# Attention scores of 20 of 32 visits: from float32 products of 64 rows to float32r products of rounded and remaining parts

## The chip, the cores and the metric

The kernel runs on one core of a Trainium2 chip. The metric is device time in microseconds (us) of one execution; the kernel before takes 1064.93 us (median of 3 runs, 1064.68 to 1065.62). The engines are called PE (TensorE; PEld is its weight load), DVE (VectorE), ACT (ScalarE), POOL (GpSimd) and SP (SyncE, which issues all the DMAs here).

## What is computed

Attention with a compressive memory for 4 batches, 8 heads, 576 tokens and 64 dimensions, and behind it two feed-forward layers over 2304 tokens of 512 values:

```python
scores = scale * np.matmul(q, k.transpose(0, 1, 3, 2))      # causal, then softmax
local = np.matmul(a, v)
mem_out = mem_ret / mem_norm                                # phi(q) against M_prev, z_prev
attn = g * mem_out + (1 - g) * local
gate = 1.0 / (1.0 + np.exp(-(x @ w_gate)))
x = gate * (x @ w_val) @ w_out                              # layer 1, d_ff 1536
h = x @ w_in
out = (h * np.clip(h + 3.0, 0.0, 6.0) / 6.0) @ w_out2       # layer 2, d_ff 2048
```

## The kernel before

The program has three phases. **Phase A** (to about 400 us) is attention with the first half of layer 1 filled in between; phase B is the rest of layer 1, phase C layer 2.

Attention goes in 32 visits, numbered v = 0 to 31. A visit is a pair of heads and a range of tokens: the first range (rg 0, 320 queries) or the second (rg 1, 256 queries against 576 keys). Visits 0 to 3 of a batch's eight are of the first range, 4 to 7 of the second. Of visits 12 to 31, which the change touches, 12 are of the second range (12 to 15, 20 to 23, 28 to 31) and 8 of the first (16 to 19, 24 to 27). A visit takes two steps t of the loop in `phase_a`.

`load_visit(v)` brings the transposed q and k of the pair into one tile `qk`, head 0 in partitions 0 to 63, head 1 in 64 to 127; there are two buffers of `qk`, so visit v + 2 is loaded into the buffer of visit v. `score_part` (L349) multiplies: for each head one matmul with 64 rows, in float32, which PE runs as two instructions. The columns per head are 448, 320 and 256 in a visit of the second range (1024), and 192 and 320 in one of the first (512), so that there are 3 or 2 score parts in a visit. In the first range a small 64 x 64 product of the diagonal block follows (L354). A score goes into a tile `s` of `ps_m`, four PSUM buffers that it shares with the layer's tiles `m`; DVE reads it with the mask and takes row minima (L329, `row_max`), ACT takes the exponentials (L367) and PE transposes them (L413, tile `t`), ACT copies them out (L415, tile `T`), PE multiplies them by v (L459, tile `pv`), ACT copies that to `xpr` (L468), and SP stores it to `xd` in DRAM (L473 to L477).

The layer's work in between is float32r: each operand is split into a rounded part, a float32r copy made by ACT (L233), and what remains, subtracted by DVE (L234), and three products replace one (`mm3`, L238 to L240), 128 rows and 312 columns each in phase A. Its input is read back from `xd` into tiles `xc` by `moe_x` (L499), two buffers; results leave through tiles `xp`, two buffers, to `x2p` (L541).

Weights come as 64-bit floats into `wst` (L147, two buffers of 8 KB a partition) and are converted by ACT and DVE with a help tile `wf` (L157 to L169). The last conversion of phase A's weights is in step 23, the second of visit 11. The staging buffers are free from there on, and the first two groups of phase B's weights are loaded into them at once.

PE's order in phase A is the order in which the code is written. The orders of ACT, DVE, POOL and SP are chosen by a scheduler from the same program when it is built. Each engine works through its order strictly: an instruction that waits holds up all that are behind it on its engine or queue.

## Time and profile before

| | |
|---|---|
| time, median of 3 | 1064.93 us |
| the profiled execution | 1065.71 us |
| its span, first to last instruction | 1063.9 us |
| mean granted clock of PE | 0.996 of full speed |
| busy PE / PEld / DVE / ACT | 98% / 84% / 61% / 51% of the span |
| DMA, mean | 155 GB/s, 164.87 MB |

The shares are means over stages with different limits: in phase A before 120 us DVE and ACT are the fullest, later PE is. A busy PE is modelled from the starts of its instructions, so that how long work takes on PE is best read from start to start. In the timeline a row's second number is its time from first start to last end; the chain of waits gives pieces that don't overlap. The visits can be found in the timeline by the columns of their scores: visit 12 begins with the 448 columns at 112.33 us, visit 15 at 142.88 us, visit 31 at 349.84 us; the last score is at 361.26 us.

### The profile page before, as it was taken

The page shows a single profiled execution, that of the slowest core. Times are in us where ns is not written, and L with a number is a line of the kernel's source. Part 1 is how long each engine was busy: PE and PEld are TensorE (multiplying, and loading weights), DVE is VectorE, ACT ScalarE, POOL GpSimd, SP SyncE. Part 2 cuts the span into 40 slices and gives each one's busy share as a digit, 9 for nine tenths or more (in the row PEclk, how much of TensorE's full clock was granted, in tenths as well). Part 3 has the DMA queues.
Part 4 walks back from the last instruction along what each step waited for, and adds up shares of the span by engine and source line. Part 5 has one row for each costly group of instructions (what it writes and reads, how often), then busy time and mean ns, then how long its engine had stood idle before and what let it go on. Part 6 is the DMA issues. An engine that isn't in the chain of part 4 may idle for free.

```text
span 1063.9 us, 16179 instructions
## 1 busy us (share of the span) xinstructions
PE 1038.0 (98%) x5904; PEld 892.6 (84%) x5904; DVE 648.3 (61%) x1549; ACT 538.6 (51%) x1165; POOL 84.2 (8%) x102
## 2 busy tenths in 40 slices
PE   6799999999999999999999999999999999999998
PEld 4467678878887899999888888888888888888886
DVE  6999755454455338888888888743454433643433
ACT  6679885566556644435444344433453433633432
POOL 2213211110111000000000000410002000000000
PEclk9899999999999999999999999999999999999999
DMA  7755642424242215337686877444414542044511
GB/s 220 223 191 184 192 126 75 137 80 124 67 126 80 64 44 180 119 119 254 228 296 246 309 259 276 158 166 177 148 30 158 218 159 99 10 168 169 218 40 59
DMA packets 66239, 164.87 MB, mean 155 GB/s; under 512 B 8432, under 2 KB 41712, under 8 KB 60272
## 3 DMA queue, kind: packets, MB, share of 16 engines
q1 hardware_dynamic: 66160, 163.85, 45.2%
q8 instruction: 46, 0.75, 0.3%
q14 instruction: 33, 0.27, 0.1%
HBM read 122.76 MB, written 41.06 MB: 154 GB/s over the span
## 4 chain that ended last, share of the span: by engine, by line
PE 89%; DVE 4%; DMA 4%; ACT 1%; SPq 1%; issue 1%; POOL 0%; ACTq 0%; DVEq 0%
PE acc L866 18%; PE pa L831 9%; PE pb L831 7%; PE m L238 6%; PE g L240 6%; PE g L238 6%; PE g L239 6%; PE m L239 5%; PE m L240 5%; PE pv L459 5%; PE t L413 4%; PE s L349 4%; PE acc L238 3%; PE acc L240 3%; PE acc L239 3%; DMA xd<-xpr 1%
## 5 line engine op out<-in xcount | busy, mean ns | idle before, releaser
L866 PE MATMUL acc<-wslot,hs 128*128 128x512 f32 x864 | 227.8, 395 | 2.2 <-ACT hs L233 2.2
L866 PEld LDWEIGHTS acc<-wslot,hs 128*128 128x128 f32 x864 | 159.5, 188 | 27.7 <-ACT hs L233 3.5
L831 PE MATMUL pa<-xq,wslot 128*128 128x384 f32 x576 | 117.3, 338 | 1.1 <-ACT u L931 0.6
L831 PEld LDWEIGHTS pa<-xq,wslot 128*128 128x128 f32 x576 | 103.7, 187 | 9.9 <-ACT u L931 0.9
L240 PE MATMUL g<-xs,wslot 128*128 128x468 f32 (+1 forms) x288 | 106.4, 370 | 0.0
L239 PE MATMUL g<-xs,wslot 128*128 128x468 f32 (+1 forms) x288 | 106.3, 369 | 0.0
L238 PE MATMUL g<-xs,wslot 128*128 128x468 f32 (+1 forms) x288 | 104.1, 369 | 0.0
L367 ACT ACTIVATE P<-P,m 128x192 f32<-128x192 f32 (+4 forms) x144 | 83.9, 585 | 28.4 <-DVE m L329 27.3
L238 PE MATMUL m<-xs,wslot 128*128 128x312 f32 x288 | 94.4, 328 | 0.4 <-ACT xs L233 0.4
L239 PE MATMUL m<-xs,wslot 128*128 128x312 f32 x288 | 88.5, 307 | 0.1
L240 PE MATMUL m<-xs,wslot 128*128 128x312 f32 x288 | 88.1, 306 | 0.0
L831 PE MATMUL pb<-xq,wslot 128*128 128x384 f32 x432 | 87.8, 338 | 0.0
L831 PEld LDWEIGHTS pb<-xq,wslot 128*128 128x128 f32 x432 | 77.9, 188 | 6.3
L349 PE MATMUL s<-qk 64*128 64x320 f32 (+3 forms) x320 | 72.5, 491 | 10.3 <-DMA qk<-in_qk 7.1
L895 DVE TENSOR_TENSOR c<-pb,u 128x384 f32<-128x384 f32 x48 | 26.6, 555 | 86.7 <-ACT u L931 85.7
L843 ACT ACTIVATE r<-c,three 128x384 f32<-128x384 f32 x72 | 44.2, 614 | 63.4 <-DVE c L895 63.4
L413 PEld LDWEIGHTS t<-ident,P 128*128 128x128 f32 x464 | 53.6, 144 | 23.2 <-issue 11.9
L234 DVE TENSOR_TENSOR hs<-r,hs 128x384 fp32r<-128x384 f32 x96 | 56.5, 593 | 26.9 <-ACT hs L233 25.4
L413 PE MATMUL t<-ident,P 128*128 128x128 f32 x464 | 67.7, 284 | 3.6 <-POOL P L382 3.5
L329 DVE CUSTOM_DVE_ANT_0 P<-s,mask 128x320 f32<-128x320 f32 (+3 forms) x144 | 62.8, 451 | 13.3 <-PE s L349 13.2
L415 ACT COPY T<-t 128x512 f32<-128x512 f32 (+2 forms) x128 | 65.9, 540 | 8.4 <-PE t L413 8.3
L157 ACT ACTIVATE wf<-wst 128x512 f32<-128x512 f32 (+1 forms) x59 | 43.9, 744 | 43.4 <-DVE wst L163 36.7
(106 smaller groups left out, 1937.9 us busy)
## 6 DMA issues: line engine op xcount, KB each, us to landing
wst<-in_wm SPq DMA_DIRECT2D x68, 512.0 KB, 5.9
wslot<-wd SPq DMA_DIRECT2D x30, 1024.0 KB, 5.1
wd<-wslot SPq DMA_DIRECT2D x16, 1024.0 KB, 4.6
wslot<-wd SPq DMA_DIRECT2D x15, 768.0 KB, 6.4
wd<-wslot SPq DMA_DIRECT2D x8, 768.0 KB, 5.8
qk<-in_qk SPq DMA_DIRECT2D x32, 160.0 KB, 2.4
aux<-in_aux SPq DMA_DIRECT2D x16, 320.0 KB, 3.8
qk<-in_qk SPq DMA_DIRECT2D x16, 288.0 KB, 3.1
```

The source lines that it names most:

```text
L234: elo.tensor_tensor(lo, src, hi.bitcast(F32), op=ALU.subtract)
L238: nc.tensor.matmul(out, w[0], x[0], start=first, stop=False)
L239: nc.tensor.matmul(out, w[0], x[1], start=False, stop=False)
L240: nc.tensor.matmul(out, w[1], x[0], start=False, stop=last)
L329: self.nc.vector.tensor_tensor_reduce(out=self.row(v, rg, r, 64 + a, 64 + e), in0=ps, in1=mask, scale=-0.125, scalar=3.0e38 if a == 0 else ...
L349: nc.tensor.matmul(ps[:, : e - a], qk[rows, 0, q0 : q0 + 128], qk[rows, 1, a:e], start=True, stop=True)
L367: self.nc.scalar.activation(x, x, AF.Exp, bias=vs["m", rg][:, r : r + 1], scale=-1.0, accum_out=vs["l", rg][:, r : r + 1])
L413: nc.tensor.transpose(ps[:, 128 * n : 128 * n + 128], self.row(v, rg, r, 128 * j, 128 * j + 128), self.ident)
L415: nc.scalar.copy(pr["T", rg][:, 512 * k : 512 * k + c], ps[:, :c])
L459: nc.tensor.matmul(ps[rows, o : o + w], pr["v"][:, j, rows], T[:, c : c + w], start=(n == 0), stop=(n == last), skip_group_check=True,)
L831: nc.tensor.matmul(ps[:, :HC], w[:, i, b, cc], x[:, l, k], start=first and k == 0 and n == 0, stop=last and k == 1 and n == 2, skip_group_ ...
L866: nc.tensor.matmul(a, h[:, i, cc], w[:, l, f], start=first and f == 0 and n == 0, stop=last and f == 1 and n == 2)
```

## The change

For visits 12 to 31 (`ROUND = 12`) the scores are made of float32r products.

- **Load.** A second input, `qkd`, holds for each head its 64 rows of q and k twice, in partitions 0 to 63 and again in 64 to 127. A visit loads two tiles `qk`, one for each head: four DMAs of twice the bytes in all. The two tiles take both buffers of `qk`, so one visit's load fills what the visit ahead of it filled.
- **Split.** `split_qk(v + 1)` runs in the first step of visit v. For each head ACT rounds the whole tile to float32r (`hi`, 640 columns in the first range and 832 in the second) and DVE subtracts twice with 64 rows: the remaining part of k into `klo` (320 or 576 columns), and that of q into the half of `hi` where q stands the second time (320 or 256 columns). `hi` lies in the buffers of `wst`, which grow to 9 KB.
- **Scores.** For each head one matmul of 128 rows gives rounded q times rounded k and remaining q times rounded k at once; then for both heads one of 64 rows gives rounded q times the remaining k.
- **Diagonal block.** It stays float32, from a tile `ends` in the place of `wf`, with a DMA of its own.
- **Room.** `xc` and `xp` share three buffers in place of two each.

```diff
+ROUND = 12
@@ load_visit
+        if v < ROUND:
+            qk = self.pa2.tile([128, 2, S], F32, name="qk", tag="qk")
+            nc.sync.dma_start(qk[:, 0, t0 : t0 + n], self.qk[b, h // 2, :, 0, t0 : t0 + n])
+            nc.sync.dma_start(qk[:, 1, : t0 + n], self.qk[b, h // 2, :, 1, : t0 + n])
+        else:
+            qk = [self.pa2.tile([128, 2 * S], F32, name="qk", tag="qk") for g in range(2)]
+            for g in range(2):
+                nc.sync.dma_start(qk[g][:, :n], self.qkd[b, h // 2, :, g, 0, t0 : t0 + n])
+                nc.sync.dma_start(qk[g][:, n : t0 + 2 * n], self.qkd[b, h // 2, :, g, 1, : t0 + n])
@@ new
+    def split_qk(self, v):
...
+        x, w = vs["qk"], t0 + 2 * n
+        hi = self.stage.tile([128, 2, 2 * S], F32R, name="hi", tag="wst")[:, :, :w]
+        lo = self.pa2.tile([128, S], F32R, name="klo", tag="klo")
+        for g in range(2):
+            nc.scalar.copy(hi[:, g], x[g][:, :w])
...
+            sub(lo[mine, : t0 + n], mine, n, w)
+            sub(hi[other, g, :n], other, 0, n)
...
+            vs["ends"] = self.stage.tile([128, 2, 64], F32, name="ends", tag="wf", bufs=1)
+            nc.sync.dma_start(vs["ends"], self.qk[b, h // 2, :, :, 0:64])
+
+    def scores(self, v, ps, g, q0, a, e):
...
+        yield nc.tensor.matmul(ps, hi[:, g, q], hi[:, g, n + a : n + e], start=True, stop=False)
+        yield nc.tensor.matmul(ps, hi[rows, g, q], lo[rows, a:e], start=False, stop=True)
@@ score_part
+        if v >= ROUND:
+            for _ in zip(*[self.scores(v, tiles[g][:, : e - a], g, q0, a, e) for g in range(2)]):
+                pass
@@ moe_x, moe_a
-            x = self.pm2.tile([128, CA], F32, name="xc", tag="xc")
+            x = self.pm2.tile([128, CA], F32, name="xc", tag="xc", bufs=3)
-            o = self.pm2.tile([128, CA], F32, name="xp", tag="xp")
+            o = self.pm2.tile([128, CA], F32, name="xp", tag="xc", bufs=3)
@@ phase_a, first step of a visit
+                self.split_qk(v + 1)
                 self.load_visit(v + 2)
```

PE's order is otherwise the same from end to end. At the first score of visit 12 it reads before (x2 stands for the two heads):

```order
L240 MATMUL m<-xs_587,wslot 128x312
L349 MATMUL s<-qk 128x448 x2
L413 MATMUL t<-ident,P 128x128 x8
L238 MATMUL m<-ha_722,wslot 128x312
L239 MATMUL m<-ha_722,wslot 128x312
```

and after (L240 to L242 are the three products of `mm3` now, L462 is the transpose):

```order
L242 MATMUL m<-xs_587,wslot 128x312
L328 MATMUL s<-hi 128x448 x2
L329 MATMUL s<-klo,hi 128x448 x2
L462 MATMUL t<-ident,P 128x128 x8
L240 MATMUL m<-ha_722,wslot 128x312
```

The one float32 pair has become a pair of 128-row products and a pair of 64-row products in the same place.

SP's queue around the change from visit 11 to visit 12, before, with what each DMA waits for. The first `qk` pair here is the load of visit 12, the second that of visit 13; `xc` is the layer's input, and the four loads of phase B's weights follow after one more visit's stores:

```order
L262 DMA qk<-in_qk 128x256 [waits DMAHW3_49,PE_49]
L263 DMA qk<-in_qk 128x576 [waits DMAHW4_49]
L265 DMA aux<-in_aux 128x320 [waits DMAHW5_49,PE_49]
L279 DMA aux<-in_aux 128x384 [waits DMAHW6_49]
L473 DMA xd<-xpr 64x320 [waits DMAHW7_49,Activation_49]
L474 DMA xd<-xpr 64x256 [waits DMAHW0_49]
L475 DMA xd<-xpr 64x64 [waits DMAHW1_49]
L499 DMA xc<-xd 128x312 [waits DMAHW7_49,DMAHW2_49,DMAHW1_49]
L262 DMA qk<-in_qk 128x256 [waits DMAHW3_49,PE_49]
L263 DMA qk<-in_qk 128x576 [waits DMAHW4_49]
```

The same stretch after. The first `qkd` pair is head 0 of visit 12, the second head 0 of visit 13, the third head 1 of visit 12:

```order
L270 DMA qk<-in_qkd 128x256 [waits DMAHW3_49,PE_49]
L271 DMA qk<-in_qkd 128x576 [waits DMAHW4_49]
L273 DMA aux<-in_aux 128x320 [waits DMAHW5_49,PE_49]
L287 DMA aux<-in_aux 128x384 [waits DMAHW6_49]
L522 DMA xd<-xpr 64x320 [waits DMAHW7_49,Activation_49]
L523 DMA xd<-xpr 64x256 [waits DMAHW0_49]
L524 DMA xd<-xpr 64x64 [waits DMAHW1_49]
L270 DMA qk<-in_qkd 128x256 [waits DMAHW3_49,DMAHW2_49,DMAHW4_49,DVE_49,Activation_49]
L271 DMA qk<-in_qkd 128x576
L270 DMA qk<-in_qkd 128x256 [waits PE_49]
L271 DMA qk<-in_qkd 128x576 [waits DMAHW5_49]
```

The load of visit 12 is in two halves, and the second stands where the load of visit 13 stood; it waits for the scores of visit 11 (PE), and a load that waits for the split of visit 12's first half (DVE) stands ahead of it. The `xc` loads and the weight loads have left this stretch.

ACT at the same place, before (from the end of the weight conversion to the first exponentials of visit 12):

```order
L168 CAST wslot<-wst 128x1024
L367 ACTIVATE P,l<-P,m 128x320
L468 COPY xpr<-pv 128x320
L367 ACTIVATE P,l<-P,m 128x320
L233 CAST xs_1685<-xc 128x312
L303 ACTIVATE phw<-phw 128x256
L233 CAST ha_1408<-th 128x312
```

and after:

```order
L170 CAST wslot<-wst 128x1024
L517 COPY xpr<-pv 128x320
L309 CAST hi<-qk 128x832
L416 ACTIVATE P,l<-P,m 128x320 x2
L235 CAST ha_1422<-th 128x312
L309 CAST hi<-qk 128x832
L345 ACTIVATE phw<-phw 128x256
```

The first `hi` here is head 1 of visit 12, the second head 0 of visit 13; the exponentials of visit 11 come behind the first, and the cast of the layer's input `xs` has moved down.

## Rows read from the trace of the kernel before

**Rows 1.** Page, part 4: shares of the chain that ended last, by engine.
```profile
PE 89%; DVE 4%; DMA 4%; ACT 1%; SPq 1%; issue 1%; POOL 0%; ACTq 0%; DVEq 0%
```

**Rows 2.** Stretches: length, busy PE, PEld, DVE, ACT, POOL, clock, DMA share, GB/s.
```profile
112.00:143.00 31.00, 28.86 (x177) 20.03 (x177) 21.11 (x75) 25.36 (x63) 6.39 (x8) 1.00 0.58 187
143.00:290.00 147.00, 147.00 (x1070) 120.67 (x1071) 74.03 (x287) 91.23 (x244) 17.17 (x28) 1.00 0.34 98
```

**Rows 3.** PE's waits: 130 to 365 us; from 365 us (total, times, longest).
```profile
PE m L239 <- DVE ha L234: 0.9, 1, 0.9
...
PE acc L866 <- ACT hs L233: 2.2, 3, 0.9
```

**Rows 4.** Chain of waits, 140 to 165 us: start, length, what.
```profile
142.96 0.95 PE s L349 x4
143.91 1.02 PE t L413 x8
...
155.60 0.53 PE s L349 x4
```

**Rows 5.** Timeline, weight loads around one score pair of 320 columns.
```profile
163.94 0.30 PEld L349 LDWEIGHTS s<-qk 64*128 64x128 f32 x4 [0.18 <-issue]
...
164.68 0.20 PEld L413 LDWEIGHTS t<-ident,P 128*128 128x128 f32 x2 [0.44 <-issue]
```

**Rows 6.** Timeline of PE, float32r products of 128 rows: 20 and 14 steps.
```profile
166.12 0.30 PE L240 MATMUL m<-xs,wslot 128*128 128x312 f32 x1
...
168.99 0.30 PE L239 MATMUL m<-xs,wslot 128*128 128x312 f32 x1
...
599.90 0.38 PE L240 MATMUL acc<-hs,wslot 128*128 128x468 f32 x1
...
602.86 0.38 PE L240 MATMUL g<-xs,wslot 128*128 128x468 f32 x1
```

**Rows 7.** Groups by shape, 143 to 365 and 60 to 125 us: busy, mean ns.
```profile
L233 ACT CAST xs<-xc 128x312 fp32r<-128x312 f32 x16 | 7.2, 452 | 4.5 <-DMA xc<-xd 4.5
...
L168 ACT CAST wslot<-wst 128x1024 fp32r<-128x1024 f32 x6 | 6.9, 1146 | 3.3 <-DVE wst L160 3.3
...
L234 DVE TENSOR_TENSOR ha<-th,ha 128x312 fp32r<-128x312 f32 x24 | 11.6, 481 | 1.1 <-ACT ha L233 1.0
...
L169 DVE TENSOR_TENSOR wslot<-wst,wslot 128x1024 fp32r<-128x1024 f32 x6 | 7.3, 1217 | 0.0
```

**Rows 8.** Timelines around visit 12's first score; landing times of the `qk` loads.
```profile
109.20 0.33 SPq L262 DMA_DIRECT2D qk<-in_qk  x1
109.58 0.42 SPq L263 DMA_DIRECT2D qk<-in_qk  x1
...
112.33 1.02 PE L349 MATMUL s<-qk 64*128 64x448 f32 x4
...
112.96 0.42 ACT L468 COPY xpr<-pv 128x320 f32<-128x320 f32 x1
...
113.95 1.19 DVE L163 CUSTOM_DVE_ANT_0 wst<-wst,wf 128x2048 uint16<-128x2048 uint16 x1
...
DMA to landing us min/median/max: 2.0/2.5/6.7
```

**Rows 9.** Chain of waits and PE's timeline, 117 to 137 us.
```profile
118.17 5.98 DMA wst<-in_wm
124.16 5.96 DMA xd<-xpr
...
130.03 0.86 PE L459 MATMUL pv<-T,aux 128*64 128x256 f32 x6 [1.61 <-ACT T L415]
...
133.57 2.13 PE L349 MATMUL s<-qk 64*128 64x448 f32 x4
```

**Rows 10.** Stretches early in phase A, with the columns of rows 2.
```profile
44.00:46.00 2.00, 1.02 (x5) 0.53 (x4) 2.00 (x8) 0.20 (x1) 0.00 (x0) 0.91 0.80 206
46.00:48.00 2.00, 2.00 (x5) 0.76 (x4) 1.13 (x5) 1.15 (x4) 0.72 (x1) 0.50 0.97 356
...
52.00:54.00 2.00, 1.61 (x12) 1.35 (x10) 1.54 (x5) 0.53 (x2) 0.00 (x0) 0.88 0.29 80
```

More of the change, by code (lines that the diff above doesn't have):

```diff
@@ L81, with __init__ @@
 class Kernel:
-    def __init__(self, tc, ctx, qk, aux, zz, bt, wm1, wm2, out):
+    def __init__(self, tc, ctx, qk, qkd, aux, zz, bt, wm1, wm2, out):
         self.tc, self.nc, self.ctx = tc, tc.nc, ctx
-        self.qk, self.aux, self.zz, self.bt = qk, aux, zz, bt
+        self.qk, self.qkd, self.aux, self.zz, self.bt = qk, qkd, aux, zz, bt
         self.wm1, self.wm2, self.out = wm1, wm2, out
@@ L256, in load_visit @@
         b, h = PAIRS[p]
-        qk = self.pa2.tile([128, 2, S], F32, name="qk", tag="qk")
         a = self.pa2.tile([128, 15 * D], F32, name="aux", tag="aux", bufs=3)
@@ L287, in load_visit @@
         }
+    def split_qk(self, v):
+        if not ROUND <= v < len(VISITS):
+            return
+        nc = self.nc
+        vs = self.visits[v]
+        t0, n = RTOK[vs["ranges"][0]]
+        x, w = vs["qk"], t0 + 2 * n
[3 more added lines that the diff above has]
+            nc.scalar.copy(hi[:, g], x[g][:, :w])
+            mine, other = slice(64 * g, 64 * g + 64), slice(64 - 64 * g, 128 - 64 * g)
+            sub = lambda o, rows, a, e: nc.vector.tensor_tensor(
+                o, x[g][rows, a:e], hi[rows, g, a:e].bitcast(F32), op=ALU.subtract
+            )
+            sub(lo[mine, : t0 + n], mine, n, w)
+            sub(hi[other, g, :n], other, 0, n)
+        vs["hi"], vs["klo"], vs["n"] = hi, lo, (t0, n)
+        if t0 == 0:
+            b, h = vs["pair"]
+            vs["ends"] = self.stage.tile([128, 2, 64], F32, name="ends", tag="wf", bufs=1)
+            nc.sync.dma_start(vs["ends"], self.qk[b, h // 2, :, :, 0:64])
+    def scores(self, v, ps, g, q0, a, e):
+        nc = self.nc
+        vs = self.visits[v]
+        rows = slice(64 * g, 64 * g + 64)
+        hi, lo, (t0, n) = vs["hi"], vs["klo"], vs["n"]
+        q = slice(q0 - t0, q0 - t0 + 128)
+        yield nc.tensor.matmul(ps, hi[:, g, q], hi[:, g, n + a : n + e], start=True, stop=False)
+        yield nc.tensor.matmul(ps, hi[rows, g, q], lo[rows, a:e], start=False, stop=True)
     def prep_phi(self, v):
@@ L344, in score_part @@
         q0, off = QB[i][0], 512 - 128 * i
-        tiles = []
-        for g in range(2):
-            rows = slice(64 * g, 64 * g + 64)
-            ps = self.ps_m.tile([128, 512], F32, name="s", tag="m")
-            nc.tensor.matmul(ps[:, : e - a], qk[rows, 0, q0 : q0 + 128], qk[rows, 1, a:e], start=True, stop=True)
-            tiles.append(ps)
+        tiles = [self.ps_m.tile([128, 512], F32, name="s", tag="m") for g in range(2)]
+        if v >= ROUND:
+            for _ in zip(*[self.scores(v, tiles[g][:, : e - a], g, q0, a, e) for g in range(2)]):
+                pass
+            if i == 1:
+                ends = self.visits[v]["ends"]
+        else:
+            ends = qk
+            for g in range(2):
+                rows = slice(64 * g, 64 * g + 64)
+                nc.tensor.matmul(
+                    tiles[g][:, : e - a], qk[rows, 0, q0 : q0 + 128], qk[rows, 1, a:e], start=True, stop=True
+                )
         if i == 1:
@@ L354, in score_part @@
                 nc.tensor.matmul(
-                    tiles[1][rows, e : e + 64], qk[rows, 0, 0:64], qk[rows, 1, 0:64], start=True, stop=True, skip_group_check=True
+                    tiles[1][rows, e : e + 64], ends[rows, 0, 0:64], ends[rows, 1, 0:64], start=True, stop=True, skip_group_check=True
                 )
@@ L992, in _arrays @@
         "qk": qk,
+        "qkd": np.ascontiguousarray(np.stack([qk[:, :, [64 * g + d for d in range(64)] * 2] for g in range(2)], axis=3)),
         "aux": aux,
```

2 lines of the change are left out of this document (removed).

## The prediction

> **What bounds the kernel now.** I read the chain of waits first: 89% of it is PE [rows 1], so a change counts through what PE does or waits for. Then the stretches [rows 2]. From 143 to 290 us, which is visits 15 to 26, PE is busy throughout, ACT 91.23 us of 147 and DVE 74.03: PE bounds, and time taken from PE is gained. From 112 to 143 us PE is busy 28.86 of 31 us only, while ACT is at 25.36 and DVE at 21.11: here PE waits, and ACT is the fullest engine behind it. PE's list of waits has one after 143 us within the attention, 0.9 us for a remaining part from DVE [rows 3]. Behind 365 us it has 3.3 us in all, the longest group 2.2 us, for ACT in phase C, and none for weights [rows 3]; as PE's order there is unchanged, what is won or lost in the attention reaches the end whole.
>
> **The scores on PE.** One pair in the chain takes 0.95 us with 448 columns and 0.53 us with 192 [rows 4]: (0.95 - 0.53) / 256 = 1.64 ns a column, and a fixed part of 0.21 us. At 2.4 GHz 1.64 ns are four passes for both heads together, so the two heads run side by side. The fixed part is seen in the weight loads [rows 5]: PE's loader stands still 0.18 us ahead of the four loads of the pair and 0.44 us ahead of the transposes behind it, so the array is emptied between products of 128 and of 64 rows and the next weights aren't loaded in advance.
>
> After the change a head first gets a product of 128 rows, of the kind of the layer's. Twenty steps of 312 columns take 168.99 - 166.12 = 2.87 us, 0.1435 each, and fourteen of 468 take 2.96 us, 0.2114 each [rows 6]: 0.435 ns a column and 0.008 us fixed, with the weights loaded meanwhile. No row shows a float32r product of 64 rows. The nearest is the float32 pair itself; one pass of four gives 1.64 / 4 = 0.41 ns a column for both heads, and the fixed 0.21 us stays, since the array still goes from 128 rows to 64 and back once for each part. So a column costs 2 x 0.435 + 0.41 = 1.28 ns in place of 1.64.
>
> Twelve visits have 1024 columns and eight have 512: 16,384. Before: 16,384 x 1.64 ns = 26.9 us. After: 21.0 us, 52 parts with two more steps each at 0.008 us, 0.8 us, and for the 16 products of 192 columns the pace of the transposes in place of 0.091 us, since weights come no faster there: 1.02 / 8 = 0.127 us [rows 4], 0.6 us. **Gain 26.9 - 21.0 - 0.8 - 0.6 = 4.5 us.** Bounds: if the 64-row pair ran one head after the other, 0.41 x 16,384 = 6.7 us more, a loss of 2.2; if the fixed part belonged to float32 and fell away, 52 x 0.21 = 10.9 us less, a gain of 15.4. I take 4.5, as the nearest rows are pairs of the same 64 rows.
>
> All rows of 64 rows are also float32, so the trace alone can't say which of the two empties the array. The Trainium skill, page "TensorEngine Tiling (Array Packing)", section "Key Properties", says that changing the tiling mode, not just the tile, drains the engine. By that rule it is the mode, the stall stays and the gain is 4.5 us; without it 15.4 us would be possible. Rows 5 agree as far as they go, with 0.18 and 0.44 us.
>
> **The split on ACT and DVE.** Casts take 0.452 us for 312 columns and 1.146 for 1024 [rows 7], so 0.96 us for 832 and 0.77 for 640: two a visit, 35 us over 20 visits. Subtractions take 0.481 and 1.217 us [rows 7]: 0.75 for 576, 0.42 for 256, 0.49 for 320; 2.3 us a visit of the second range and 2.0 of the first, 44 us in all. From 143 to 290 us about 12 splits fall: ACT goes from 91 to 112 us of 147 (76%), DVE from 74 to 100 (68%). PE's work hides them. If that cover fails, it is by order: four subtractions are 2.3 us in a row on DVE, behind which row minima and the layer's `th` and `ha` wait, and PE waits for the PSUM buffers that these free. The trace has one such wait of 0.9 us [rows 3]. Lower bound none, upper bound 0.9 us in each of the 17 visits from 15 on, 15 us; I take two or three more of that size, **2.0 us lost**, since over 147 us PE waited for nothing.
>
> **The change from visit 11 to visit 12.** Up to here a visit loaded into the buffer of two visits ago. Visit 12 needs both buffers, and the second is read by visit 11's last score. Its load goes where SP issued visit 13's, at 109.20 us [rows 8], but behind two issues for visit 13 (0.33 + 0.42) and its own two: 110.7. Landing took 2.0 to 6.7 us, median 2.5 [rows 8]; with twice the bytes under way I take 2.9: 113.6. Then the cast, 0.96: 114.6 (the copy ahead of it on ACT began at 112.96 [rows 8]). DVE is by then in the 1.19 us of L163, which began at 113.95 [rows 8] and will begin later, because visit 12's first half put 1.17 us on a full DVE: 115.4. Two subtractions, 1.17 us: 116.5. PE began that score at 112.33 [rows 8]. **4.2 us lost**, 2.5 with the shortest landing and an idle DVE (109.95 + 0.75 + 2.0 + 0.96 + 1.17 = 114.8), 7.2 with the longest landing. Later visits load into buffers that their predecessor's split frees a visit ahead, some 10 us, against 2.5 for landing and 4.3 for casts and subtractions: no loss.
>
> Behind a thin stretch of PE the granted clock went to 0.50, 1.2 GHz, for some 6 us [rows 10]: after 1.02 us of work in 2 us. A wait of 4 us may do the same; half speed for 6 us costs 3. Between 0 and 3 I take **1.0 us lost**.
>
> **What goes with the old loads.** In the kernel before, 2 MB of phase B's weights are fetched at 117 us; the chain goes through them for 5.98 us, through a store for 5.96 us, and PE waits 1.61 us for a copy on ACT and takes 2.13 us for a score of 448 columns that takes 1.02 elsewhere [rows 9, 8]. Now these buffers hold `hi`, the weights come after the attention, `xc` comes later in SP's queue, and a PE that is 4 us late finds the copies done: **2.7 us gained** (1.61 + 1.11; 0 at least). The conversion of half a group that was done early moves behind the attention, some 3 us on DVE there; that PE waits for no weights from 365 us on [rows 3] is its cover, and it would cost up to 3 us without.
>
> The small edits cost nothing as I see it: the `ends` load waits on SP for the diagonal product that PE has done by then, and the three shared buffers free as the stores and splits did; behind either wait the stores to `xd` would queue, whose readers come a visit later.
>
> **Sum.** -4.5 + 2.0 + 4.2 + 1.0 - 2.7 = 0.0 us: the profiled execution would stay at 1065.71 us, and the median, 0.78 below it, at **1064.9 us**.
>
> **The rivals.**
> - *The switch alone is paid.* No new waits and no fall of the clock: -4.5 + 4.2 - 2.7 = -3.0, 1061.9 us; with the short landing 1060.2. For it: PE's clean 147 us. Against: ACT at 25.36 of 31 us from 112 to 143 us, with 6 us of casts to come.
> - *The array isn't emptied for float32r.* 10.9 us less: 1054.0 us. For it: all stalled rows are float32. Against: transposes are float32 too, of 128 rows, and run at 0.127 us without a stall ahead.
> - *Slower: DVE's blocks hold PE.* A layer tile is 12 steps, 1.72 us, and its PSUM buffer comes round three tiles later. Once DVE is further behind than the tiles between the scores give it, each visit loses some 0.4 us: 17 x 0.4 = 6.8 in place of 2.0, 1069.7 us. For it: splits of 2.3 us in a row; against: DVE at 68%.
> - *Slower: "both at once" isn't.* If 64-row float32r products run one after the other, 6.7 us more: 1071.6 us. Against: the float32 pairs do run together.
>
> **How the numbers follow.** The balance as summed, 0.38; the switch alone, 0.22; no emptying, 0.10; DVE's blocks, 0.20; one after the other, 0.10. A measurement of this kernel tells 0.2%, 2.1 us, from no change. Faster 0.22 + 0.10 = 0.32, same 0.38, slower 0.20 + 0.10 = 0.30. The likeliest alone holds 1062.8 to 1067.1. The range goes from 1059.5, below the short landing, to 1071.0: it leaves out the case without emptying, half of the last case and the tail of DVE's, some 2 in 10.
>
> **What would show it.** In the profile after: pieces of scores of 0.20 us for each 448-column product of 128 rows and 0.40 us for the 64-row pair with its fixed part; twice that slope would show the pair apart, a load of weights without a pause ahead of it the missing stall. A wait of PE of about 4 us ahead of visit 12's first score, released by DVE, and clock rows of 0.50 behind it or not. No PE wait for a copy near 130 us. From visit 15 to 31 PE's waits should sum to some 2 us. The forecast is wrong if the time from visit 15's first score to the last one, 142.88 to 361.26 us before, doesn't shrink by 1 to 3 us, or if phase B waits for weights.

## The result, and the profile after

The changed kernel takes **1073.9 us** (median of 4 runs, 1073.4 to 1077.5), beside 1065.3 for the kernel before on the same chip: ratio 1.0085, 95% interval 1.0064 to 1.0106. Forecast were 1064.9 us, within a range up to 1071.0. The change costs 9 us where a balance of nought was expected.

The page of the kernel after: busy time by engine, and the chain's shares by engine.

```profile
PE 1039.5 (97%) x5904; PEld 907.4 (85%) x5904; DVE 691.5 (65%) x1629; ACT 565.1 (53%) x1205; POOL 89.1 (8%) x102
...
PE 85%; DVE 6%; DMA 4%; ACT 2%; issue 1%; SPq 1%; POOL 0%; ACTq 0%; DVEq 0%
```

PE's share of the chain fell from 89% to 85% [rows 1]; DVE's rose from 4% to 6% and ACT's from 1% to 2%. Where, PE's list of waits from 95 to 380 us says (total, times, longest):

```profile
PE s L328 <- DVE hi L311: 4.0, 1, 4.0
PE m L241 <- DVE xs L236: 2.5, 2, 2.3
PE m L241 <- DVE ha L236: 0.9, 2, 0.7
PE m L240 <- ACT ha L235: 0.8, 1, 0.8
PE pv L508 <- ACT T L464: 0.7, 1, 0.7
```

Its stretches, with the columns of rows 2:

```profile
112.00:125.00 13.00, 9.04 (x45) 7.82 (x41) 11.93 (x31) 10.52 (x24) 3.69 (x6) 0.74 0.59 169
125.00:143.00 18.00, 17.30 (x116) 13.62 (x115) 12.34 (x41) 15.08 (x35) 2.34 (x3) 1.00 0.61 178
143.00:165.00 22.00, 19.45 (x138) 15.83 (x138) 16.13 (x56) 19.29 (x47) 2.35 (x4) 1.00 0.52 153
165.00:290.00 125.00, 124.76 (x911) 108.47 (x908) 83.57 (x284) 88.34 (x224) 17.57 (x26) 1.00 0.47 132
```

Against rows 2: PE is still full behind 165 us, but from 112 to 143 us it is idle for 4.7 us in place of 2.1 (with the clock at 0.74 in the first part), and from 143 to 165 us for 2.5 us in place of nothing.

PE's order is nearly the same in all these kernels, so the surest way to read the two traces is to subtract starts. The table takes the first `pv` product of a visit in PE's timeline and gives its start less that in the kernel before, in us, for the kernels that the explanation needs most (they are told of below). A trace is one execution; the times of one kernel lie up to 8 us apart.

| first `pv` product of visit (its start before, us) | after | `unshare` | `third_room` | `split_only` | `unshare_third` | `no_loads` | `ring3` |
|---|---|---|---|---|---|---|---|
| 8 (100.62) | +1.54 | +0.24 | -2.21 | -0.94 | -1.82 | +0.92 | -1.88 |
| 10 (117.11) | +8.37 | +6.73 | -2.24 | -0.42 | -1.44 | +1.25 | -1.91 |
| 11 (127.24) | +7.01 | +6.61 | +0.29 | +0.95 | +2.29 | +4.91 | +2.23 |
| 12 (144.86) | +4.46 | +3.38 | +0.16 | +4.24 | +3.19 | +1.30 | -1.61 |
| 13 (157.34) | +7.43 | +3.26 | +4.40 | +5.04 | +3.01 | +1.11 | -1.55 |
| 24 (294.92) | +6.60 | +1.08 | +2.94 | +5.57 | +1.28 | -0.24 | -2.86 |
| 25 (308.24) | +8.78 | +3.75 | +3.66 | +6.79 | +2.00 | +0.42 | -2.15 |
| 31 (386.09) | +7.57 | +2.52 | +2.43 | +6.89 | +1.13 | -0.81 | -3.39 |

In the column of the kernel after there are three steps up, at visit 12's scores (+6.8), at visit 16's (+3.0) and at 308 us (+2.2), one recovery (-3.9, visits 10 to 12), and a slow slope down. The 1.5 us at visit 8 arise in the start-up, where the orders on all engines are still equal. The profiled execution of `never`, a kernel told of below, took 2560.3 us in place of the 1064.9 to 1067.8 of its eleven others, so its trace is not in the table.

**First step, +6.8.** Timelines of PE, ACT and DVE around visit 12's scores (PE's rows first), and in a second fence three stretches of the same kernel behind them:

```profile
113.90 0.37 PE L328 MATMUL s<-hi 128*128 128x448 f32 x1
118.23 0.71 PE L328 MATMUL s<-hi 128*128 128x448 f32 x1 [3.96 <-DVE hi L311]
...
114.68 0.89 ACT L309 CAST hi<-qk 128x832 fp32r<-128x832 f32 x1
114.82 1.64 DVE L165 CUSTOM_DVE_ANT_0 wst<-wst,wf 128x2048 uint16<-128x2048 uint16 x1
116.88 0.75 DVE L311 TENSOR_TENSOR klo<-qk,hi 64x576 fp32r<-64x576 f32 x1
117.67 0.42 DVE L311 TENSOR_TENSOR hi<-qk,hi 64x256 fp32r<-64x256 f32 x1
```

```profile
118.00:120.00 2.00, 1.77 (x5) 1.03 (x6) 2.00 (x7) 0.70 (x1) 0.00 (x0) 0.50 0.62 120
120.00:122.00 2.00, 2.00 (x11) 2.00 (x10) 2.00 (x7) 1.80 (x6) 0.72 (x1) 0.50 0.33 126
122.00:124.00 2.00, 2.00 (x10) 1.96 (x9) 1.10 (x4) 2.00 (x6) 0.73 (x1) 0.50 0.15 27
```

Head 1's product waits 3.96 us for the subtractions, as the prediction said step by step. But then the clock is at 0.50 (1.2 GHz) from 118 to 124 us: 6.8 - 4.0 leaves 2.8 us for it, where the forecast has 1.0.

**Second step, +3.0.** This one stands nowhere in the prediction. DVE's and PE's timelines at visit 16:

```profile
155.70 0.29 DVE L344 TENSOR_SCALAR phw<-aux 128x256 f32<-128x256 f32 x1 [2.36 <-DMA aux<-in_aux]
155.91 0.48 DVE L236 TENSOR_TENSOR xs<-xc,xs 128x312 fp32r<-128x312 f32 x1
...
156.44 0.41 PE L241 MATMUL m<-xs,wslot 128*128 128x312 f32 x1 [2.29 <-DVE xs L236]
```

The layer works through its tokens in chunks of 312, and PE is about to begin chunk 1 and needs the last part of its input; its subtraction stands on DVE behind `phw`, and `phw` waits 2.36 us for an `aux` load. In the kernel before DVE waits at the same `phw` too, 3.02 us at 149 us, but the last of the four `xs` was subtracted at 141.37 us. Why they are late now is seen on SP. The loads of chunk 1's input, before (four rows) and after (two rows of two):

```profile
107.51 0.33 SPq L499 DMA_DIRECT2D xc<-xd  x1
116.38 0.33 SPq L499 DMA_DIRECT2D xc<-xd  x1
130.26 0.33 SPq L499 DMA_DIRECT2D xc<-xd  x1
138.44 0.33 SPq L499 DMA_DIRECT2D xc<-xd  x1
```

```profile
140.97 1.06 SPq L548 DMA_DIRECT2D xc<-xd  x2
147.57 0.80 SPq L548 DMA_DIRECT2D xc<-xd  x2
```

Before, an `xc` was loaded as soon as a visit had stored its part. Now all four come 9 to 33 us later, with 4 to 10 us left until PE wants them at 151 us. `xc` and `xp` share a ring of three buffers, and a ring hands its buffers out in the order of the program: the loads stand behind the stores of `xp`.

**Third step, +2.2.** At the next boundary between chunks, 307 us, PE waits 0.77 us for `ha` from ACT and 0.73 from DVE, where it waited once for 0.9 before [rows 3], and the clock drops again (timeline, then one stretch):

```profile
306.89 0.41 PE L240 MATMUL m<-ha,wslot 128*128 128x312 f32 x1 [0.77 <-ACT ha L235]
308.03 0.41 PE L241 MATMUL m<-ha,wslot 128*128 128x312 f32 x1 [0.73 <-DVE ha L236]
```

```profile
309.00:311.00 2.00, 2.00 (x12) 1.54 (x12) 2.00 (x6) 0.14 (x2) 1.48 (x3) 0.50 0.83 287
```

This step needs no splits. `neither` (told of below) leaves out 18 of the 20, waits 1.49 us at the same place, and loses 2.3 us between visits 24 and 25 (-4.86 to -2.55 us):

```profile
296.58 0.41 PE L244 MATMUL m<-ha,wslot 128*128 128x312 f32 x1 [1.49 <-DVE ha L239]
```

### The profile page after: what moved, and what is told of

The parts are those of the page before. It is cut to its first block, busy times and chain, and to the rows that moved or that the text cites. A ratio compares the mean times of both kernels' runs of the same rounds, so it can differ in the third digit from the quotient of the medians.

```text
span 1071.7 us, 16444 instructions
## 1 busy us (share of the span) xinstructions
PE 1039.5 (97%) x5904; PEld 907.4 (85%) x5904; DVE 691.5 (65%) x1629; ACT 565.1 (53%) x1205; POOL 89.1 (8%) x102
## 4 chain that ended last, share of the span: by engine, by line
PE 85%; DVE 6%; DMA 4%; ACT 2%; issue 1%; SPq 1%; POOL 0%; ACTq 0%; DVEq 0%
PE acc L916 18%; PE pa L881 9%; PE pb L881 7%; PE g L242 6%; PE g L240 6%; PE g L241 6%; PE m L240 5%; PE m L241 5%; PE m L242 5%; PE pv L508 4%; PE t L462 4%; PE acc L240 3%; PE acc L242 3%; PE acc L241 3%; PE s L329 1%
## 5 line engine op out<-in xcount | busy, mean ns | idle before, releaser
L242 PE MATMUL g<-xs,wslot 128*128 128x468 f32 (+1 forms) x288 | 106.4, 370 | 0.0
L240 PE MATMUL g<-xs,wslot 128*128 128x468 f32 (+1 forms) x288 | 104.1, 369 | 0.0
L240 PE MATMUL m<-xs,wslot 128*128 128x312 f32 x288 | 94.7, 329 | 1.8 <-ACT xs L235 1.8
L242 PE MATMUL m<-xs,wslot 128*128 128x312 f32 x288 | 88.4, 307 | 0.0
L462 PE MATMUL t<-ident,P 128*128 128x128 f32 x464 | 70.4, 291 | 2.9 <-POOL P L431 2.9
L462 PEld LDWEIGHTS t<-ident,P 128*128 128x128 f32 x464 | 55.8, 149 | 14.8 <-issue 8.1
L508 PE MATMUL pv<-T,aux 128*64 128x256 f32 (+2 forms) x512 | 62.9, 374 | 2.9 <-ACT T L464 2.8
```

Source lines behind the costliest of these rows:

```text
L240: nc.tensor.matmul(out, w[0], x[0], start=first, stop=False)
L242: nc.tensor.matmul(out, w[1], x[0], start=False, stop=last)
L462: nc.tensor.transpose(ps[:, 128 * n : 128 * n + 128], self.row(v, rg, r, 128 * j, 128 * j + 128), self.ident)
L508: nc.tensor.matmul(ps[rows, o : o + w], pr["v"][:, j, rows], T[:, c : c + w], start=(n == 0), stop=(n == last), skip_group_check=True,)
```

## The experiments

All were timed in five rounds beside the kernel before, which took 1065.4 to 1065.9 us on these chips.

| kernel | what it is | median, us | ratio to before, 95% interval |
|---|---|---|---|
| `never` | after, no visit in the new form | 1066.2 | 1.0007, 0.9998 to 1.0016 |
| `third_room` | after, own buffer for visit 12's second half | 1069.0 | 1.0046, 1.0029 to 1.0063 |
| `aux_first` | after, aux loads ahead of q and k | 1078.6 | 1.0121, 1.0107 to 1.0135 |
| `round28` | after, switch at visit 28 | 1067.8 | 1.0020, 1.0010 to 1.0029 |
| `pe_alone` | `third_room`, two visits loaded and split | 1059.1 | 0.9934, 0.9921 to 0.9946 |
| `split_only` | `third_room`, float32 scores | 1073.1 | 1.0068, 1.0055 to 1.0081 |
| `late` | `third_room`, q and k loaded half a visit later | 1069.3 | 1.0034, 1.0024 to 1.0044 |
| `ring3_late` | `late`, ring of three buffers | 1069.3 | 1.0039, 1.0024 to 1.0054 |
| `unshare` | after, own rings for xc and xp | 1068.9 | 1.0025, 1.0015 to 1.0035 |
| `unshare_third` | `third_room` with own rings | 1069.1 | 1.0032, 1.0017 to 1.0048 |
| `unshare_third20` | the same, switch at visit 20 | 1064.3 | 0.9987, 0.9973 to 1.0001 |
| `neither` | `unshare_third`, two visits loaded and split | 1060.8 | 0.9945, 0.9930 to 0.9960 |
| `no_loads` | `unshare_third`, splits without loads | 1062.4 | 0.9972, 0.9960 to 0.9984 |
| `no_splits` | `unshare_third`, loads without splits | 1083.9 | 1.0165, 1.0147 to 1.0183 |
| `ring3` | `unshare_third`, ring of three buffers | 1062.2 | 0.9976, 0.9963 to 0.9989 |
| `ring3_20` | the same, switch at visit 20 | 1061.7 | 0.9965, 0.9953 to 0.9977 |
| `ring3_old` | `ring3`, no visit in the new form | 1064.0 | 0.9984, 0.9975 to 0.9993 |

### First: the start-up, the switch, SP's order

The theory was that 1.5 us belong to the start-up, 6.8 to the buffer of visit 12's second half, and 2.5 to SP, where `aux` loads stand behind q and k loads that wait for splits.

```diff
 # never, round28
-ROUND = 12
+ROUND = 32    # or 28
 # third_room: q and k packed to 832 columns, and
+            last = dict(tag="qkx", bufs=1) if v == ROUND else dict(tag="qk")
+            qk = [self.pa2.tile([128, QW], F32, name="qk", **(last if g else dict(tag="qk"))) for g in range(2)]
 # aux_first: the q and k loads of load_visit moved behind its aux loads
```

> The changed code with the switch put behind the last visit, so that no visit uses the new form. What is left of the change: xc and xp share one ring of three buffers, and one more input array lies in memory. Question: the 1.5 to 1.7 us by which the changed kernel is already late at visits 9 to 11, where the order on every engine is still that of the kernel before. Theory A (that lateness is chance of the start-up's clock in the one profiled execution, or goes with the parts not built here): 1065.3 us, within 0.2% of the kernel before. Theory B (the shared ring or the layout costs it): about 1.6 us above the kernel before, 1066.9.

> The changed kernel, but visit 12's second half (head 1) has a buffer of its own, so that it no longer waits until visit 11's scores have read theirs; to make room, a visit's q and k stand packed side by side (832 columns a buffer). Theory A (the 4.0 us wait on TensorE at visit 12's first scores comes from that buffer, and the fall of the granted clock to 0.50 behind it comes from the wait): the wait falls to under 1 us and no window from 118 to 126 us has a clock under 0.9; the time falls by 4 to 7 us, to about 1068 (all of the 6.8 us lost between visits 11 and 12, less what later waits had taken up anyway). Theory B (the two splits and the last weight conversion, queued on VectorE and ScalarE, hold the scores by themselves): the wait stays over 2 us and the time within 2 us of 1073.9.

> The changed kernel, but a visit's aux loads are issued on SP ahead of its q and k loads, so that they don't queue behind loads that wait for the split of the visit before. Theory A (the 2.3 us wait of TensorE for xs at 156 us comes from VectorE standing at phw until that aux load has landed, and the xs subtraction behind it): that wait is gone, the time falls by 2 to 3 us, to about 1071.4. Theory B (the xc load, or VectorE's own work, ends as late anyway): the wait stays over 1.5 us under another name and the time within 1 us of 1073.9.

> The changed kernel with the switch at visit 28 instead of 12: the last four visits alone, all of the shape 128x192 and 128x448, take the new form. By the change's trace these four gain about 0.3 us each. Theory A (the cost is one for each switch: a wait of about 4 us at the first visit of the new form and the clock fall behind it, 3 us; the gain goes with the number of visits): 1065.3 - 1.2 + 4 to 7, that is 1068 to 1071. Theory B (the cost is spread over the 20 visits, by splits, loads and their queues): 4/20 of 8.6, about 1067.

`never` is within 0.1% of the kernel before. The start-up's 1.5 us are no price of the change: in the traces of the other kernels, `aux_first` left out, visit 8 stands between -3.3 and +2.4 us, and `round28`, late by 2.4 us at visit 7, is late by 0.08 at visit 12, since PE has waits in the kernel before [rows 9] that take lateness up. `never` says one thing more: the shared ring alone, without splits, costs 0.8 us at the most likely (interval -0.2 to 1.7).

`third_room` took 4.9 us off, as much as its first theory had said, but both signs of that theory failed: the wait of 4.0 us became two, 0.9 and 1.2, and a fall of the clock stayed (stretches):

```profile
120.00:122.00 2.00, 0.81 (x4) 0.34 (x4) 1.64 (x5) 2.00 (x6) 0.22 (x1) 1.00 0.73 212
122.00:124.00 2.00, 2.00 (x11) 1.72 (x11) 1.55 (x7) 1.69 (x5) 0.51 (x1) 0.54 0.73 155
124.00:126.00 2.00, 2.00 (x12) 1.99 (x11) 1.87 (x7) 1.96 (x7) 0.97 (x1) 0.61 0.41 147
```

`aux_first` missed. It moved the very first visit's loads too, and lost 8 us in the start-up, which hides the rest; but the wait for `xs` was there still, with 3.2 us, so the order of `aux` against q and k is not its cause. `round28` came out between its two forecasts. Its step, +3.4 us, is at visit 25's `pv` near 308 us, where its switch meets the chunk's boundary.

### Second: the products alone, the split alone

```diff
 # pe_alone: only visits 12 and 16 are loaded and split; later ones take their parts
+        if v not in (ROUND, ROUND + 4):
+            of = self.visits[ROUND + 4 * (v // 4 % 2 == 0)]
+            vs.update({key: of[key] for key in ("hi", "klo", "n", "ends") if key in of})
+            return
 # split_only: one float32 product of 64 rows for a head
-        yield nc.tensor.matmul(ps, hi[:, g, q], hi[:, g, n + a : n + e], start=True, stop=False)
-        yield nc.tensor.matmul(ps, hi[rows, g, q], lo[rows, a:e], start=False, stop=True)
+        x = hi[rows, g].bitcast(F32)
+        yield nc.tensor.matmul(ps, x[:, q], x[:, n + a : n + e], start=True, stop=True)
 # late, ring3_late: load_visit brings aux alone, q and k come in a second call half a visit later
```

> The kernel third_room, but q and k are loaded and split for visits 12 and 16 only; the other 18 visits of the new form score with these parts (their own q and k are left out, so their scores are not theirs). What stands on TensorE is unchanged; ScalarE, VectorE, SP and the DMA rings are freed of 18 splits and 72 loads. Theory A (the products themselves are worth about 3 us over the 20 visits, 0.3 a visit of the 128x192 and 128x448 shapes and 0.1 to 0.2 of the others; what third_room still loses, at visit 16 and at the chunk boundary near 307 us, comes from splits and loads): 1063 to 1065, and no wait over 1 us after visit 12. Theory B (the new products bring the later waits by themselves, since they feed VectorE and ScalarE in pairs): over 1067, with the wait for xs near 150 us still there.

> The kernel third_room, but the scores of the 20 visits are one float32 product of 64 rows for each head, as in the kernel before, read from the rounded parts (the products with the remaining parts are left out). Loads and splits are all there. Theory A (products worth about 3 us): 1072, 3 us above third_room's 1069.0. Theory B (the float32r form of the products is worth the 4.5 us of the prediction, or more): 1073.5 or above. Theory C (worth nothing): 1069.

> The kernel third_room, but a visit's q and k loads of the new form are issued on SP half a visit later, when the split that frees their buffers has been queued for half a visit; its aux loads stay where they were. Theory A (SP stands at q and k loads that wait for the split, and the aux and xd loads behind them come late; that is the wait of 1.9 us for xs near 152 us, and the fall of the clock behind it): VectorE no longer stands over 1 us at phw near 150 us, and the time falls by 2 to 4 us, to 1065 to 1067. Theory B (VectorE and ScalarE are late by their own work): the wait moves to another name, the time stays within 1 us of 1069.

> The kernel late, with the third buffer in one ring for all visits rather than kept for visit 12. Now visits 12 and 13 need no buffer of the visit before theirs. Theory A (the rest of the loss at the switch, about 2.5 us in third_room, is SP waiting at visit 13's loads for visit 11's buffer): 1 to 2.5 us under late, about 1064, under the kernel before. Theory B (it is the work of the two splits beside the last weight conversions on VectorE and ScalarE): the same as late within 1 us.

The new form's products are worth what was forecast. They can be read on PE itself, from the start of the instruction ahead of a score part to the start of the one behind. A part of 448 columns, before (113.28 - 112.10 = 1.18 us) and after (148.30 - 147.25 = 1.05 us):

```profile
112.10 0.30 PE L240 MATMUL m<-xs,wslot 128*128 128x312 f32 x1
112.33 1.02 PE L349 MATMUL s<-qk 64*128 64x448 f32 x4
113.28 1.09 PE L413 MATMUL t<-ident,P 128*128 128x128 f32 x8
```

```profile
147.25 0.31 PE L242 MATMUL m<-ha,wslot 128*128 128x312 f32 x1
147.40 0.57 PE L328 MATMUL s<-hi 128*128 128x448 f32 x2
147.90 0.47 PE L329 MATMUL s<-klo,hi 64*128 64x448 f32 x2
148.30 0.87 PE L462 MATMUL t<-ident,P 128*128 128x128 f32 x6
```

Over the parts behind 160 us that have no wait the gain is 0.135 us with 448 columns, 0.10 with 320, 0.08 with 256 and 0.03 with 192. Twelve visits of the second range and eight of the first make 4.8 us of that. The runs agree. From visit 13 to 31 `split_only` loses 1.85 us on the kernel before and `third_room` gains 1.97 (table above): 3.8 us between kernels whose program differs in the products alone (0.5 of it at the boundary of 308 us). By the medians it is 4.1, between the first two theories of `split_only`. The 16 visits scored there have 12,288 of the 16,384 columns, for which the prediction's 4.5 us give 3.4. `pe_alone`, at 1059.1 under both its forecasts, is 6.4 us under the kernel before, and 9.9 under `third_room`: that much hangs on splits and loads. `late` and `ring3_late` changed nothing, as their second theories had it; in `late` DVE still stands 3.63 us at `phw`, the wait for `xs` stayed in both (2.8 and 2.6 us), and with it the theory fell that SP's waits for splits cause it. What all kernels so far with a wait for that input share is the ring of `xc` and `xp`.

### Third: own rings

```diff
-            x = self.pm2.tile([128, CA], F32, name="xc", tag="xc", bufs=3)
+            x = self.pm2.tile([128, CA], F32, name="xc", tag="xc")
-            o = self.pm2.tile([128, CA], F32, name="xp", tag="xc", bufs=3)
+            o = self.pm2.tile([128, CA], F32, name="xp", tag="xp")
-        hi = self.stage.tile([128, 2, 2 * S], F32R, name="hi", tag="wst")[:, :, :w]
+        hi = self.stage.tile([128, 2, 832], F32R, name="hi", tag="wst")[:, :, :w]
```

> The changed kernel, but xc and xp have a ring of two buffers each again, as in the kernel before (the room comes from the hi tile, 832 columns a head instead of 1152); nothing else. In the changed kernel SP loads chunk 1's four xc tiles at 141 to 148 us, in the kernel before at 107 to 138 us, since in the shared ring they stand behind chunk 0's xp stores. Theory A (the late inputs put the xs subtractions behind phw and its aux load on VectorE; TensorE's wait of 2.3 us at visit 16, and the waits at the next boundary near 307 us, come from that): no wait for xs over 0.5 us, and the time falls by 3 to 6 us, to 1068 to 1071; the wait of about 4 us for visit 12's scores stays. Theory B (the loads are late because SP stands at q and k loads): the wait for xs stays over 1.5 us and the time within 1.5 us of 1073.9.

> Both mends at once: a buffer of its own for visit 12's second half, and own rings for xc and xp. Theory A (these two are what turned the change into a loss; the products' 4 us are then left over): neither the 4 us wait at visit 12 nor a wait for xs over 0.5 us, and third_room's 1069.0 less 4 to 6 us: 1063 to 1065, at or under the kernel before. Theory B (splits and loads cost by their work on VectorE and ScalarE): 1068 to 1070.

> The kernel unshare_third with the switch at visit 20 instead of 12, behind the last weight conversions and between the chunk boundaries near 150 and 307 us. Theory A (what still costs at the switch is the crowd of VectorE and ScalarE near 120 us): no wait over 1 us at visit 20's scores; twelve visits gain 0.15 to 0.3 us each, 2 to 3 us: 1062 to 1063.5. Theory B (a switch costs about 2.5 us wherever it stands): 1065 to 1066.

`unshare` takes 5.0 us off, as its first theory had it. Its list of PE's waits from 95 to 380 us has no `xs` any more, and the rest as it was:

```profile
PE s L328 <- DVE hi L311: 4.0, 1, 4.0
PE m L241 <- DVE ha L236: 1.2, 1, 1.2
PE pv L508 <- ACT T L464: 0.8, 1, 0.8
PE m L240 <- ACT ha L235: 0.8, 1, 0.8
...
```

SP loads `xc` at 107.88, 116.84, 133.15 and 142.31 us there, and visit 16's step is gone from the table (+3.0 after, -0.1 here; 1.3 more of the 5.0 lie in the start-up of the two traces). That `never` has the shared ring at 0.8 us and `unshare` gains 5.0 by doing without shows a price of more than one cause: late inputs cost only where little time is left for them. `round28` loads them in two pairs as well, at 135.60 and 141.70 us, without splits at that time; its four `xs` are done by 146.1 us, and PE doesn't wait. The order that the scheduler chose for DVE is part of it too: `split_only` has the ring and the splits, but its last `xs` stands ahead of `phw` (152.53 and 156.40 us), and PE doesn't wait for it either.

But the two mends don't add: `unshare_third` is no faster than either, as its second theory had it. With the switch at visit 20 the time is 1064.3 us, between the two forecasts. Most of what is left sits at 115 to 135 us: from visit 8 to visit 12 `unshare_third` loses 5.0 us on the kernel before, and `unshare_third20` gains 1.4. There ScalarE's and PE's timelines of `unshare_third` have these rows, and SP's the load that ACT waits for:

```profile
121.23 0.33 SPq L274 DMA_DIRECT2D qk<-in_qkd  x1
121.61 0.43 SPq L275 DMA_DIRECT2D qk<-in_qkd  x1
...
125.80 0.89 ACT L313 CAST hi<-qk 128x832 fp32r<-128x832 f32 x1 [1.65 <-DMA qk<-in_qkd]
...
133.26 0.86 PE L513 MATMUL pv<-T,aux 128*64 128x256 f32 x6 [2.56 <-ACT T L469]
```

Visit 13's load was issued when visit 12's split had freed its buffer; ACT stands 1.65 us at the rounding until it has landed, all that is queued behind on ACT comes late, the last copy of `T` too, and PE waits 2.56 us; behind it the granted clock is 0.57 from 134 to 138 us. This is the wait of 1.61 us [rows 9] again, which after the change had shrunk to 0.70 us (at 136.14 us) only because PE was later still.

### Fourth: splits or loads, order or bytes

```diff
 # neither: as pe_alone, on unshare_third.   no_splits: that without leaving out loads
 # no_loads
+        elif v > ROUND:
+            qk = self.visits[ROUND]["qk"]
 # ring3, ring3_20, ring3_old (ROUND = 12, 20, 32)
-            qk = [self.pa2.tile([128, QW], F32, name="qk", **(last if g else dict(tag="qk"))) for g in range(2)]
+            qk = [self.pa2.tile([128, QW], F32, name="qk", tag="qk", bufs=3) for g in range(2)]
```

> The kernel unshare_third, but q and k are loaded and split for visits 12 and 16 only; the other 18 visits of the new form score with those parts (their own q and k are left out). This is pe_alone (1059.1) with own rings for xc and xp. Theory A: pe_alone's wait of 1.2 us for xs goes too, 1057 to 1058.5. Theory B (own rings cost something while VectorE and ScalarE convert the last weights near 120 us): 1060 or above.

> The kernel unshare_third, but from visit 13 on the splits read visit 12's q and k, and no more q and k are loaded (the scores of these visits are not theirs). All splits stay on ScalarE and VectorE; SP and the DMA rings are freed of the loads, and of SP's waits for splits. Theory A (what is left of the loss after both mends, about 10 us against the products alone, comes from the splits' work on the two engines beside the last conversions near 120 us): within 2 us of unshare_third's 1069.1. Theory B (it comes from the loads, through SP's order and the DMA engines): 1058 to 1062. Theory C (both): between.

> The kernel unshare_third, but only visits 12 and 16 are split, and the other 18 visits of the new form score with those parts; all q and k are loaded. ScalarE and VectorE are freed of 18 splits; no load waits for a split. Theory A (splits' work): 1058 to 1062. Theory B (loads by the bytes they move, twice those of the kernel before): within 2 us of 1069.1. Theory C: between.

> The kernel unshare_third with its third buffer in one ring for all visits, so that the first half of each visit's q and k is loaded without waiting for the split of the visit before. In unshare_third ScalarE stands 1.65 us at visit 13's first rounding, whose load was issued only at 121.2 us, behind the split of visit 12; the last copy of T comes late behind it and TensorE waits 2.6 us at 133 us. Theory A (the loop split, buffer, load, next split is what is left of the loss): ScalarE's wait for that load is under 0.5 us, TensorE's wait for T falls by 1.5 us or more, and the time is 1065.5 to 1067.5. Theory B (the DMA engines are full there, or the splits' own work does it): within 1 us of 1069.1.

> The kernel ring3 with the switch at visit 20. In unshare_third20 ScalarE stands 1.65 us at visit 20's second rounding, waiting for its load, at 205 us. Theory A: that wait goes, and the time is 0.5 to 1.5 us under unshare_third20's 1064.3, under the kernel before beyond the spread. Theory B: 1064 to 1065.

> The kernel ring3 with the switch behind the last visit: all 32 visits keep the float32 scores, and only the packed q and k, the ring of three buffers and the own rings for xc and xp are left. Theory A (what ring3 and ring3_20 gain against the kernel before, 3.2 and 3.7 us, comes from the new form's products): within 1.2 us of the kernel before, and 3 us above ring3. Theory B (it comes from the third buffer, which lets the old form load earlier too): 1062 or under, as ring3.

Splits without loads cost 1.7 us by the medians (`no_loads` less `neither`; 2.9 by the ratios, and the two intervals touch), the loads 6.7 more (`unshare_third` less `no_loads`), so that the second theory of `no_loads` comes nearest. `neither` was forecast at 1058.5 or less, or 1060 or more; that own rings cost something, its second theory, isn't shown by 1.7 us more than `pe_alone`, since the intervals overlap. `no_splits` settles nothing: its tiles have no reader, so a load waits for the one before into the same buffer, 15 times on SP in one stretch of 70 us,

```profile
SPq L274 <- DMA qk<-in_qkd: 12.4, 15, 2.1
```

and SP's other transfers wait behind. `ring3` then moves the same bytes as `unshare_third`, but the first half of a visit's load finds a free buffer. It gains 6.9 us (6.0 by the ratios), more than its first theory had forecast. PE's waits from 95 to 380 us:

```profile
PE s L331 <- ACT P L454: 1.3, 1, 1.3
PE s L331 <- DVE hi L314: 1.2, 1, 1.2
PE m L245 <- DVE wslot L174: 0.9, 1, 0.9
PE m L243 <- ACT ha L238: 0.8, 1, 0.8
PE m L244 <- DVE ha L239: 0.7, 1, 0.7
...
```

No `pv` waits for `T`, and the table shows it: of the 4.1 us lost between visits 10 and 11, 3.8 are given back by visit 12, where `unshare_third` gives nothing back. So it is the order, the loop of split, buffer, load and next split, not the bytes.

`ring3_20` beats both kernels, 0.35% under the kernel before (interval 0.23 to 0.47%), and by more than was forecast. `ring3_old`, between its forecasts, shows that 1.7 us of that come without any new products, from the third buffer, the packing and the own rings together. Where they come from is open: in its trace, which is its fastest run, 3.3 us arise ahead of visit 8 and 0.2 behind it. The rest, some 2 us (0.4 to 3.6 by the two intervals), is what remains of the products' gain over twelve visits, 3.0 us by the readings on PE.

## Why the prediction was wrong, by its own steps

- **Scores on PE, -4.5: right,** 4.8 by the readings on PE; for visits 16 to 31 alone 3.4 us were due and 3.8 measured between kernels. The pair of 64 rows runs side by side: it takes 0.40 us with 448 columns (147.90 to 148.30) and 0.31 with 256 (146.12 to 146.43), 0.47 ns a column for both heads, where one head after the other would have taken twice 0.41 or more. The array is still emptied around it: PEld stands still 0.31 us ahead of the pair's weights and 0.21 ahead of the transposes', in place of 0.18 and 0.44 [rows 5]. So the rivals "array isn't emptied" and "both at once isn't" fall. The Trainium skill ("TensorEngine Tiling (Array Packing)", "Key Properties") says that a change of the tiling mode drains the engine; the trace agrees for float32r as well, with these pauses.

```profile
147.90 0.19 PEld L329 LDWEIGHTS s<-klo,hi 64*128 64x128 f32 x2 [0.31 <-issue]
148.30 0.86 PEld L462 LDWEIGHTS t<-ident,P 128*128 128x128 f32 x8 [0.21 <-issue]
```

- **Waits from the split on ACT and DVE, +2.0: near in size, by luck.** The splits' work costs 1.7 us (`no_loads` less `neither`), but not as two or three waits from visit 15 on. In the traces `neither` gains 2.6 us from visit 10 to visit 12, and `no_loads`, with the splits, nothing: the price falls at the switch, and behind visit 12 `no_loads` is the one that gains more (2.1 us to 0.8). The waits at 307 us in the trace after are no price of the splits, since `neither` waits there as long. The rival of DVE's blocks in each visit falls: from 165 to 290 us PE is busy 124.76 of 125 us.
- **The switch, wait +4.2: right,** 3.96. **The clock behind it, +1.0: too small,** 2.8; the row that it was taken from [rows 10] shows 0.50 after a PE busy for 1.02 us of 2, and PE did nothing at all from 116 to 118 us here. The upper end of its 0 to 3 us was right.
- **What goes with the old loads, -2.7: it came, for another reason.** The trace gives 3.9 us back by visit 12; 0.8 of it would be the products of three visits. But the wait for `T` shrank because PE was late, as the last clause of that step said, and not with the old loads: in `third_room` and `unshare_third`, where PE isn't late, it is back with 1.26 and 2.56 us, behind the new loads, and in `round28`, where the weights' loads are gone from there and of the rest only the shared ring is at work yet, it is 1.16 us. A term that is earned by being late can't be kept once the lateness is mended; that is in part why the two mends didn't add. The cover for phase B's weights held: behind 365 us PE waits 3.3 us in all, as before.
- **Later visits' loads, "no loss": wrong, but hidden.** They were to have some 10 us, since the split of the visit ahead frees their buffer in time. In the kernel after ACT already stands 1.03 us at 130.73 us for such a load, behind which PE, being late, waits little. Once it isn't late, the loop costs up to the 6.9 us that `ring3` gives back.
- **The small edits, 0: this step failed,** and without its 3.0 to 5.0 us the time would lie inside the range. It asked when the shared buffers come free, and who reads the `xd` stores behind a wait. It didn't ask what a shared ring does to the loads that come next in it. Those of chunk 1's input had been issued from 107 us on, and stand now behind chunk 0's `xp` stores: 3.0 us at visit 16 in the trace, 5.0 us by the times (`unshare`). SP's order showed it before any run: before the change the `xc` loads stand singly between visits' loads, and after it in two pairs. The step on the old loads even says that `xc` comes later in SP's queue, and counts it with the gains; when PE needs it was not asked.

The account of the trace: start-up +1.5; switch +6.8 (forecast 5.2); given back -3.9 (forecast 2.7 and the products of three visits); late inputs +3.0 (forecast 0); products -0.8 to visit 24 and -1.2 behind 308 us; boundary +2.2 (no term for it; the 2.0 for waits behind the splits was forecast within the visits). That is 7.6 us, the table's last row. The two profiled executions lie 7.7 us apart, 1073.44 and 1065.71; the 8.6 us of the medians are within the spread of the runs. The stretch that was to shrink by 1 to 3 us runs from visit 15's first score to the last one; it holds the late inputs and the boundary, and grew by 3 us.

What stays open: the waits of 1.2 to 1.3 us at visit 12's scores that `ring3` still has, why the start-up differs by some us between kernels of the same order there, and how much of each difference comes from the orders that the scheduler chose anew for ACT, DVE, POOL and SP in each kernel, since no run holds these fixed.

## What to carry to other kernels

When two kinds of tile are put into one ring, each waits for the other in program order: look in the order of the queue that fills them for loads that used to run ahead, and ask how much lead they lose and what has moved into it. A load whose buffer is freed by the step that the load feeds next runs in a loop, and one more buffer was worth more here (6.9 us) than the products that the change was made of (4.8). And a gain that a trace shows behind a new wait is counted only once the wait is gone.

## What the runs showed of the hardware

The granted clock fell to 0.50 not only behind the wait of 4.0 us but also, in `third_room`, behind waits of 0.4 and 1.9 us at 150 to 152 us. Behind a single wait of 1.61 us [rows 9] it stayed at 1.00 in the kernel before, and in `pe_alone` behind one of 1.23. Where it fell, the loss was nearly twice the wait: 6.8 us for 4.0 at visit 12 of the kernel after, 4.2 for 2.3 at visit 16 of `third_room`. It isn't settled by the length of the waits alone: behind the wait of 2.29 us at 156.44 us of the kernel after it stayed at 1.00 (the stretches from 143 to 290 us), and behind the one of 1.49 us in `neither` it was 0.50 from 299 to 301 us. Two waits of 0.77 and 0.73 us at 307 us had 0.50 behind them in the kernel after, and two of 0.8 and 0.7 us at the same place of `ring3` left it at 1.00 (the stretches from 290 to 315 us).
